# A rational activation in a fused attention and expert kernel: the absolute value moves behind a product, and unit 4 converts two weight chunks

## Chip, cores and metric

The kernel runs on one core of a Trainium2 chip. The metric is the device time of one execution in microseconds (us), as the median of several runs. Half a per cent of it is 3.1 us.

## What is computed

Causal attention over 4 batches, 12 heads, 448 positions and 64 dimensions gives x, of 1792 tokens and 768 features. On it follows a feed-forward layer with 2048 hidden features and a rational activation:

```python
h = x @ w_in
h2 = h * h
h3 = h2 * h
P = a[0] + a[1] * h + a[2] * h2 + a[3] * h3
Q = 1.0 + np.abs(b[0]) * np.abs(h) + np.abs(b[1]) * h2
g = P / (Q + 1e-06)
return (g @ w_out).astype(np.float32)
```

The weights and a, b come as 64-bit floats, and the kernel itself turns the weights into 32-bit ones. Each matrix product is made of three passes over high and low halves of the operands (fp32r): high by high, high by low, low by high.

## The kernel before

**Stages.** The first 140 us or so are attention, worked in 24 pairs of heads from an order written out by hand (ORDER, FIRST). A second written order (TAIL) leads over into the expert layer, whose first two units it contains. From unit 2 on a loop (line 674) does the rest.

**Units.** The tokens are four chunks of 512, 512, 384 and 384 columns. A unit t is one token chunk with one block f of 128 hidden features; there are 64, in the order of w_units (line 94): chunk 0 with blocks 0 to 7 (units 0 to 7), chunk 1 with all 16 (units 8 to 23), chunk 0 with blocks 8 to 15 (units 24 to 31), then chunks 2 and 3.

- p1(t) (line 198): 18 matmuls into a PSUM tile h, two buffers deep.
- act_a(t) (line 436): ScalarE reads h three times: u = |h| (L441), w = |b1 h| (L442) and p, a linear function of h (L443).
- dve_a, dve_a3 (lines 446, 453): VectorE makes w = (w + |b0|) * u (L448), and p = p * h (L451), p = (p + ..) * h (L456); L456 is the last reader of h.
- act_b (line 460): the reciprocal on ScalarE as Ln (L463) and Exp (L466), into u.
- dve_b, dve_b3 (lines 468, 477): one Newton step and the product with p (L470, L473, L479).
- g_hi, g_lo (lines 483, 488): ScalarE casts the high half gh (L485), VectorE subtracts for the low half gl (L492).
- p2(t) (line 497): 24 matmuls (18 for the shorter chunks) into psO and psM. At the last unit of a token chunk the passes are sorted so that the results come out one after another, and gl is wanted early.

In TensorE's queue p1(t+1) stands ahead of p2(t-1) in turn t of the loop.

**Weights.** Each 64-bit block of 128 rows is a chunk of the conversion; there are 32, listed in items (line 111). conv_step makes a chunk in four steps: 1 on GpSimd (L135, into a buffer u, three deep), 2 on VectorE (L145), 4 on ScalarE (L143), 3 on VectorE (L151). A chunk's raw block has three buffers, and its load is asked for when the chunk three before it is done (conv_load after conv_store, line 717). Ten chunks are converted in the attention stage; from unit 2 on there is one per unit (line 673), so chunk m is converted in unit m - 8.

Before use a 32-bit block is split: w_hi casts on ScalarE (L179), w_lo subtracts (L187) on GpSimd for w_out blocks (n == 1) and on VectorE for w_in blocks. The w_in block of unit t + 3 is split at the end of turn t. The w_out block of unit t is split in turn t, and there are two places for it:

```python
                late = (w_units[t][1], 1) in [items[m] for m in now]
                if not late and t < NU - 2:
                    split_w(t, 1)
```

stands behind dve_a3 and ahead of act_b; a late one stands at line 714, behind the conversion's step 3 and dve_b3, ahead of split_w(t + 3, 0) and so ahead of g_hi(t) and g_lo(t), which the next turn issues. By items, chunks 13, 14, 15 are the w_out blocks 5, 6, 7, and chunks 29, 30, 31 are the w_out blocks 13, 14, 15: units 5, 6, 7 and 21, 22, 23 take the late place.

SP issues all DMAs in program order: the store of a converted chunk waits for its L151, the store of split halves (L190) for L187, loads of later weights (L166, L170) stand behind them.

Of the kernel before, what the change touches and what calls it, by code (L numbers as in the profile page):

```python
# [11 lines left out]
AF = mybir.ActivationFunctionType  # L12
ALU = mybir.AluOpType
# [27 lines left out]
def kernel(  # L41
# [11 lines left out]
    nc = tc.nc  # L53
# [29 lines left out]
    bb = const.tile([P, 2], F32, name="bb")  # L83
# [72 lines left out]
    def conv_store(m):  # L156
        nc.sync.dma_start(out=w32[items[m]], in_=c_32[m])
        stored.add(items[m])
# [37 lines left out]
    h_t = {}  # L196
# [41 lines left out]
    def half(j):  # L238
        return slice(j * D, (j + 1) * D)
# [176 lines left out]
    def parse(order):  # L416
        plan = []
        for w in order.split():
            name, _, lag = w.partition("@")
            name, *arg = name.split(".")  # L420
            plan.append((tasks[name], [int(x) for x in arg], int(lag) if lag else None))
        return plan
# [7 lines left out]
    NU = len(w_units)  # L430
    tmp, g_t, acc, osb, part = {}, {}, {}, {}, {}

    def n_of(t):
        return chunks[w_units[t][0]][1]

    def act_a(t):
        h, n = h_t[t], n_of(t)
        u = tp.tile([P, 512], F32, tag="u", name="u")[:, :n]
        w = tp.tile([P, 512], F32, tag="w", name="w")[:, :n]
        pp = tp.tile([P, 512], F32, tag="p", name="p")[:, :n]  # L440
        nc.scalar.activation(out=u, in_=h, func=AF.Abs)  # L441
        nc.scalar.activation(out=w, in_=h, func=AF.Abs, scale=bb[:, 1:2])  # L442
        nc.scalar.activation(out=pp, in_=h, func=AF.Identity, scale=na[:, 3:4], bias=na[:, 2:3])  # L443
        tmp[t] = (u, w, pp)

    def dve_a(t):
        u, w, pp = tmp[t]
        nc.vector.scalar_tensor_tensor(  # L448
            out=w, in0=w, scalar=bb[:, 0:1], in1=u, op0=ALU.add, op1=ALU.mult
        )  # L450
        nc.vector.tensor_tensor(out=pp, in0=pp, in1=h_t[t], op=ALU.mult)  # L451

# [7 lines left out]
    def act_b(t):  # L460
        u, w, pp = tmp[t]
        r = u
        nc.scalar.activation(  # L463
            out=r, in_=w, func=AF.Ln, scale=2.0 ** -LSH, bias=lnb[:, 0:1]
        )
        nc.scalar.activation(out=r, in_=r, func=AF.Exp, scale=-1.0, bias=lnb[:, 1:2])  # L466
# [10 lines left out]
    def dve_b3(t):  # L477
        w, pp = tmp[t][1:]
        nc.vector.scalar_tensor_tensor(  # L479
            out=pp, in0=w, scalar=2.0, in1=pp, op0=ALU.subtract, op1=ALU.mult  # L480
        )
# [94 lines left out]
    def coeffs():  # L576
        nc.sync.dma_start(out=ab[:, 0:4], in_=moe_a.partition_broadcast(P))
        nc.sync.dma_start(out=ab[:, 4:6], in_=moe_b.partition_broadcast(P))

    def coeffs_done():  # L580
        nc.vector.tensor_scalar_mul(na, ab[:, 0:4], -1.0)
        nc.scalar.activation(out=bb, in_=ab[:, 4:6], func=AF.Abs)
# [9 lines left out]
    with tc.manual_schedule():  # L592
        nc.scalar.preload_act_table_set("natural_log_exp_and_others")
        nc.vector.memset(lnb[:, 0:1], QC * 2.0 ** -LSH)
        nc.vector.memset(lnb[:, 1:2], -LSH * LN2)
        make_identity(nc, ident)


        es_l, es_r = ExitStack(), ExitStack()
        pool = tc.tile_pool  # L600
        ep = es_l.enter_context(pool(name="ep", bufs=1))
        at = es_l.enter_context(pool(name="at", bufs=1))
        sm = es_l.enter_context(pool(name="sm", bufs=4))
        lv = es_l.enter_context(pool(name="lv", bufs=2))
        ps_t = es_l.enter_context(pool(name="ps_t", bufs=1, space=PSUM))
        ld = es_r.enter_context(pool(name="ld", bufs=2, side="right"))
        qk = es_r.enter_context(pool(name="qk", bufs=2, side="right"))
        ps_s = es_r.enter_context(pool(name="ps_s", bufs=1, space=PSUM, side="right"))
        mask = qk.tile([P, S], F32, tag="mask", bufs=1, name="mask")
        nc.gpsimd.memset(mask, 0.0)  # L610
        for x in range(2):
            m = mask[half(x), S - QB:]
            nc.gpsimd.affine_select(
                out=m, in_=m, compare_op=ALU.is_ge, fill=-1e9 / SCALE, base=0, pattern=[[-1, QB]], channel_multiplier=1,
            )
        for x in ("x3", "d"):
            ps_s.tile([P, 512], F32, tag=x, name="psS")

        V = [lv.tile([P, 2, 4, D], F32, tag=f"v{x}", bufs=1, name=f"vraw{x}") for x in range(3)]
        E = [  # L620
            [ep.tile([P, min((w + P - 1) // P * P, S)], F32, tag=f"e{x}{i}", name=f"e{x}{i}") for i, w in enumerate(b_w)]
            for x in range(2)
        ]

        warm = E[1][6][:, :P]
        idle = ps_s.tile([P, 512], F32, tag="d", name="psI")[:, :P]
        for x in range(2):
            SUM[x] = sm.tile([P, NE, 2], F32, tag=f"sum{x}", bufs=1, name="sums")
            nc.gpsimd.memset(SUM[x][:, :, 1:], 1e-9)
        for x in range(3):  # L630
            nc.gpsimd.memset(V[x][:QB, :, 3], 0.0)
        for x in range(2):
            for e, w in zip(E[x], b_w):
                if w < e.shape[1]:
                    nc.gpsimd.memset(e[:, w:], 0.0)

        nc.vector.memset(warm, 0.0)

        def keep_warm(n):
            for _ in range(n):  # L640
                nc.tensor.matmul(idle, warm, warm, start=True, stop=True, skip_group_check=True)

        keep_warm(8)

        def attend(p, part):
            for fn, arg, lag in part:
                if 0 <= p - lag < NP:
                    fn(p - lag, *arg)

        for fn, arg, p in parse(HEAD):  # L650
            fn(*arg) if p is None else fn(p, *arg)
        for p in range(NHEAD, NP):
            if p == 2:
                coeffs()
            if p == 6:
                coeffs_done()
            if p in (1, 2, 3):
                conv_load((1, 2, 3).index(p))
            attend(p, (first, second)[p] if p in (0, 1) else plan)
            if 0 <= p - NP + 4 < NL:  # L660
                conv_store(p - NP + 4)
            if p == NP - 2:
                split_w(0, 0)
            if p == NP - 2:
                load_w(0, 1)
            if p == NP - 1:
                load_w(3, 0)
                load_w(1, 1)

        for fn, arg, lag in parse(TAIL):  # L670
            fn(*arg) if lag is None else fn(NP - lag, *arg)
        todo = list(range(NC, len(items)))
        step = {t: [todo.pop(0) for _ in range(1) if todo] for t in range(2, NU)}
        for t in range(2, NU + 1):
            now = step.get(t, [])
            if t < NU - 2:
                p1(t + 1)
            g_hi(t - 1)
            g_lo(t - 1)
            if t < NU:  # L680
                dve_a(t)
                dve_a3(t)
                for m in now[:1]:
                    conv_step(m, 2)
# [3 lines that stand above are left out]
                if t + 4 < NU and splits(t + 4, 0):  # L688
                    load_w(t + 4, 0)
                if t + 3 < NU and not splits(t + 3, 0):  # L690
                    load_w(t + 3, 0)
                act_b(t)
                for m in now:
                    conv_step(m, 4)
            if t == NU - 3:
                p1(NU - 1)
            ahead = 1 < t < NU and w_units[t - 1][0] != w_units[t][0]
            if ahead:
                dve_b(t)
                dve_b3(t)  # L700
            p2(t - 1)
            if t + 1 < NU:
                act_a(t + 1)
            if NU - 2 <= t < NU:
                split_w(t, 1)
            if t < NU:
                if not ahead:
                    dve_b(t)
                for m in now[:1]:
                    conv_step(m, 3)  # L710
                if not ahead:
                    dve_b3(t)
            if t < NU and late:
                split_w(t, 1)
            if t + 3 < NU:
                split_w(t + 3, 0)
            for m in now:
                conv_store(m)
                conv_load(m + NR)
            load_w(t + 2, 1)  # L720
            for m in step.get(t + 1, []):
                conv_step(m, 1)
# [32 lines left out]
```

## Time and profile before

| | us |
|---|---|
| median of 3 runs | 629.04 |
| lowest and highest | 626.59, 629.29 |
| the profiled execution | 627.17 |
| its span, first to last instruction | 625.4 |

| engine | busy share of the span |
|---|---|
| TensorE, matmuls | 98% |
| VectorE | 83% |
| ScalarE | 69% |
| GpSimd | 29% |

In the rows below PE is TensorE's matmuls, DVE VectorE, ACT ScalarE, POOL GpSimd. L448 is line 448 of the kernel. Busy shares are averages over stages: attention up to some 140 us, the units with conversion up to some 360 us, and the rest. "out<-in" gives the tiles by their names in the program; psH is h of p1, psO and psM the two parts of p2's output, whl a split weight. [...]

### The profile page before, as it was taken

Reading aid. Unit: us, or ns where it says so; the run is one execution under the profiler, and the core shown is the slowest. Engines: PE = TensorE matmul, PEld = TensorE weight load, DVE = VectorE, ACT = ScalarE, POOL = GpSimd, SP = SyncE. Lnnn points to the kernel's source line nnn. Section 1 sums busy time; section 2 is a strip of 40 time slices with the busy share of each in tenths; the row PEclk is TensorE's granted clock in tenths of the full one; section 3 lists DMA queues with packets and bytes.
Section 4 is the critical chain, followed back from the end, with each engine's and each line's share of the span. In section 5 each row is a group of like instructions: output and inputs, shape, how many; then the busy total and the mean of one; then the engine's idle time right before and its main releaser. Section 6 shows DMA issues by size and latency. Waiting matters only on the chain.

```text
span 625.4 us, 13037 instructions
## 1 busy us (share of the span) xinstructions
PE 612.3 (98%) x4728; PEld 515.8 (82%) x4728; DVE 516.1 (83%) x1039; ACT 429.7 (69%) x940; POOL 184.3 (29%) x251
## 2 busy tenths in 40 slices
PE   7999999999999989999999999999999999999997
PEld 5666677767888768888888788899999999999996
DVE  4799999995999999999998888678766566876664
ACT  5999999996776666668776575555654555755453
POOL 3688888885643231213442300000000000000000
PEclk9899999999999989999999999999999999999999
DMA  8898888895565789888975699547477767567763
GB/s 167 227 210 189 219 205 207 220 249 170 203 252 202 273 298 323 291 303 301 324 265 214 259 373 339 211 153 288 138 249 255 271 207 255 193 201 253 253 202 126
DMA packets 108897, 149.10 MB, mean 238 GB/s; under 512 B 70945, under 2 KB 83361, under 8 KB 108833
## 3 DMA queue, kind: packets, MB, share of 16 engines
q1 hardware_dynamic: 108832, 148.27, 73.2%
q8 instruction: 37, 0.61, 0.4%
q14 instruction: 28, 0.22, 0.1%
HBM read 111.28 MB, written 36.96 MB: 237 GB/s over the span
## 4 chain that ended last, share of the span: by engine, by line
PE 76%; DVE 11%; ACT 7%; issue 4%; POOL 1%; DMA 1%; ACTq 0%; DVEq 0%; POOLq 0%
PE psH L204 29%; PE psO L528 20%; PE psM L524 11%; PE psS L288 6%; PE psD L366 5%; PE psC L342 3%; ACT e L309 3%; DVE whl L187 2%; ACT whl L179 2%; PE psA L256 2%; DVE u L145 2%; DVE gl L492 1%; DVE w L448 1%; DVE u L151 1%; DVE p L473 1%
## 5 line engine op out<-in xcount | busy, mean ns | idle before, releaser
L204 PE MATMUL psH<-xh,whl 128*128 128x512 f32 (+1 forms) x768 | 176.1, 364 | 0.5 <-DVE p L456 0.4
L528 PE MATMUL psO<-whl,gh 128*128 128x512 f32 x448 | 160.5, 394 | 1.6 <-ACT gh L485 1.5
L204 PEld LDWEIGHTS psH<-xh,whl 128*128 128x128 f32 x768 | 136.0, 188 | 16.6 <-DVE p L456 1.0
L524 PE MATMUL psM<-whl,gh 128*128 128x256 f32 x448 | 126.5, 283 | 0.0
L463 ACT ACTIVATE u<-w,lnb 128x512 f32<-128x512 f32 (+1 forms) x64 | 42.9, 671 | 105.1 <-DVE w L448 105.1
L528 PEld LDWEIGHTS psO<-whl,gh 128*128 128x128 f32 x448 | 84.5, 189 | 20.3 <-ACT gh L485 2.6
L204 PE MATMUL psH<-xl,whl 128*128 128x512 f32 (+1 forms) x384 | 87.5, 362 | 0.0
L323 POOL TENSOR_SCALAR e<-e,r 128x192 f32<-128x192 f32 (+6 forms) x168 | 77.2, 483 | 32.5 <-DVE r L319 15.4
L524 PEld LDWEIGHTS psM<-whl,gh 128*128 128x128 f32 x448 | 85.0, 190 | 1.4
L528 PE MATMUL psO<-whl,gl 128*128 128x512 f32 x224 | 81.7, 393 | 2.3 <-DVE gl L492 2.3
L309 ACT ACTIVATE e<-psS,nm 128x448 f32<-128x448 f32 (+6 forms) x168 | 77.4, 485 | 4.5 <-DVE nm L299 3.8
L204 PEld LDWEIGHTS psH<-xl,whl 128*128 128x128 f32 x384 | 70.1, 188 | 7.6
L187 DVE TENSOR_TENSOR whl<-w,whl 128x768 fp32r<-128x768 f32 x41 | 47.1, 1149 | 30.8 <-ACT whl L179 30.8
L492 DVE TENSOR_TENSOR gl<-p,gh 128x384 fp32r<-128x384 f32 (+1 forms) x62 | 41.6, 671 | 35.0 <-ACT gh L485 35.0
L441 ACT ACTIVATE u<-psH 128x512 f32<-128x512 f32 (+1 forms) x64 | 34.5, 539 | 48.8 <-PE psH L204 48.7
L299 DVE CUSTOM_DVE_ANT_0 psS<-psS,mask 128x64 f32<-128x64 f32 (+6 forms) x168 | 65.2, 453 | 2.8 <-PE psS L288 2.8
L524 PE MATMUL psM<-whl,gl 128*128 128x256 f32 x224 | 63.4, 283 | 0.0
L135 POOL TENSOR_SCALAR u<-raw 128x768 f32<-128x768 f32 x32 | 48.3, 1510 | 43.5 <-DMA raw<-in_moe_w_in_dram 16.4
L470 DVE SCALAR_TENSOR_TENSOR w<-w,u 128x512 f32<-128x512 f32 (+1 forms) x64 | 46.4, 724 | 11.3 <-ACT u L466 11.3
L448 DVE SCALAR_TENSOR_TENSOR w<-w,bb,u 128x512 f32<-128x512 f32 (+1 forms) x64 | 46.4, 725 | 6.7 <-ACT w L442 6.7
L528 PEld LDWEIGHTS psO<-whl,gl 128*128 128x128 f32 x224 | 42.3, 189 | 11.7 <-DVE gl L492 2.9
L288 PE MATMUL psS<-qkt 64*64 64x192 f32 (+6 forms) x672 | 48.7, 395 | 1.9 <-ACT e L309 1.6
(64 smaller groups left out, 992.9 us busy)
## 6 DMA issues: line engine op xcount, KB each, us to landing
whl<-whl SPq DMA_DIRECT2D x88, 768.0 KB, 4.3
w<-w SPq DMA_DIRECT2D x52, 384.0 KB, 5.4
raw<-in_moe_w_in_dram SPq DMA_DIRECT2D x16, 768.0 KB, 5.7
raw<-in_moe_w_out_dram SPq DMA_DIRECT2D x16, 768.0 KB, 4.9
w<-u SPq DMA_DIRECT2D x29, 384.0 KB, 3.4
qraw<-in_q_dram SPq DMA_DIRECT2D x48, 112.0 KB, 3.8
kraw<-in_k_dram SPq DMA_DIRECT2D x48, 112.0 KB, 3.8
out_dram<-osb SPq DMA_DIRECT2D x13, 384.0 KB, 2.9
```

Source lines behind the costliest of these rows:

```text
L135: nc.gpsimd.tensor_scalar(out=u.bitcast(F32), in0=y, scalar1=0.0, scalar2=1.0, op0=ALU.mult, op1=ALU.mult)
L187: eng.tensor_tensor(out=w[:, 1], in0=src, in1=w[:, 0].bitcast(F32), op=ALU.subtract)
L204: nc.tensor.matmul(ps, w[:, c * P:(c + 1) * P], x[c][:, lo:lo + n_tok], start=(c == 0 and n == 0), stop=(c == KD - 1 and n == 2),)
L288: nc.tensor.matmul(pss[p, b][half((1 + b + j) % 2)], QK[p][half(j), 0, b * QB:(b + 1) * QB], QK[p][half(j), 1, :b_w[b]], start=True, stop= ...
L299: nc.vector.tensor_tensor_reduce(out=s, in0=s, in1=mask[:, S - w:], scale=-SCALE, scalar=3e38, op0=ALU.add, op1=ALU.min, accum_out=nmx[p][ ...
L309: nc.scalar.activation(out=E[p % 2][i][:, :w], in_=pss[p, i], func=AF.Exp, bias=nmx[p][:, i:i + 1], scale=-1.0, accum_out=SUM[p % 2][:, i, ...
L323: nc.gpsimd.tensor_scalar(out=e, in0=e, scalar1=REC[p][:, i:i + 1], scalar2=0.0, op0=ALU.mult, op1=ALU.add)
L448: nc.vector.scalar_tensor_tensor(out=w, in0=w, scalar=bb[:, 0:1], in1=u, op0=ALU.add, op1=ALU.mult)
L470: nc.vector.scalar_tensor_tensor(out=w, in0=w, scalar=QC, in1=r, op0=ALU.add, op1=ALU.mult)
L492: eng.tensor_tensor(out=gl, in0=pp, in1=gh.bitcast(F32), op=ALU.subtract)
L524: nc.tensor.matmul(acc["m", k], g, w[:, 512:], start=first and (k % 2 == 0 or nk < 4), stop=last, skip_group_check=True)
L528: nc.tensor.matmul(acc[k], g, w[:, :512], start=first, stop=last)
```

## The change

act_a no longer makes u = |h|. L448 multiplies (w + |b0|) by h itself, read from PSUM, and ScalarE takes the absolute value of that product, in place, ahead of the logarithm: (|b1 h| + |b0|) |h| is the absolute value of (|b1 h| + |b0|) h. Unit 4 gets two chunks to convert, so that every chunk from 13 on is converted one unit earlier, and the last in unit 22 where it was 23. The second chunk's steps on VectorE (2 and 3) stand behind dve_b3 of unit 4; its step 1 on GpSimd follows the first one's at the end of unit 3, and its step 4 on ScalarE the first one's.

```diff
@@ act_a
-        nc.scalar.activation(out=u, in_=h, func=AF.Abs)
         nc.scalar.activation(out=w, in_=h, func=AF.Abs, scale=bb[:, 1:2])
@@ dve_a
-            out=w, in0=w, scalar=bb[:, 0:1], in1=u, op0=ALU.add, op1=ALU.mult
+            out=w, in0=w, scalar=bb[:, 0:1], in1=h_t[t], op0=ALU.add, op1=ALU.mult
@@ act_b
         r = u
+        nc.scalar.activation(out=w, in_=w, func=AF.Abs)
@@ the loop over units
-        step = {t: [todo.pop(0) for _ in range(1) if todo] for t in range(2, NU)}
+        step = {t: [todo.pop(0) for _ in range(1 + (t == 4)) if todo] for t in range(2, NU)}
...
                 if not ahead:
                     dve_b3(t)
+                for m in now[1:]:
+                    for n in (2, 3):
+                        conv_step(m, n)
             if t < NU and late:
                 split_w(t, 1)
```

## Rows read from the trace of the kernel before

**Rows 1.** Chain of waits: start us, us, engine, tile and line; psH blocks.
```profile
245.40 4.09 PE psH L204 x18
...
328.00 4.11 PE psH L204 x18
...
362.12 4.09 PE psH L204 x18
```
**Rows 2.** TensorE's timeline, 197 to 230 us: start, duration, instruction [idle before, releaser].
```profile
197.28 1.53 PE L204 MATMUL psH<-xh,whl 128*128 128x512 f32 x6
...
201.38 0.39 PE L528 MATMUL psO<-whl,gh 128*128 128x512 f32 x1
...
210.83 0.50 PE L528 MATMUL psO<-whl,gh 128*128 128x512 f32 x1 [0.74 <-ACT gh L485]
...
215.63 1.66 PE L204 MATMUL psH<-xh,whl 128*128 128x512 f32 x6 [0.36 <-DVE p L456]
...
223.55 0.50 PE L528 MATMUL psO<-whl,gl 128*128 128x512 f32 x1 [1.47 <-DVE gl L492]
...
224.73 0.63 PE L528 MATMUL psO<-whl,gl 128*128 128x512 f32 x1
...
228.69 1.55 PE L204 MATMUL psH<-xh,whl 128*128 128x512 f32 x6
```
**Rows 3.** Windows: busy PE, PEld, DVE, ACT, POOL; granted clock, DMA share, GB/s.
```profile
225.00:250.00 25.00, 25.00 (x120) 21.20 (x120) 24.59 (x35) 18.01 (x29) 3.91 (x3) 0.94 0.89 310
```
**Rows 4.** VectorE's timeline, units 5 to 10.
```profile
193.53 0.74 DVE L448 SCALAR_TENSOR_TENSOR w<-w,bb,u 128x512 f32<-128x512 f32 x1
...
200.30 2.03 DVE L187 TENSOR_TENSOR whl<-w,whl 128x768 fp32r<-128x768 f32 x1 [1.04 <-ACT whl L179]
...
203.54 0.74 DVE L448 SCALAR_TENSOR_TENSOR w<-w,bb,u 128x512 f32<-128x512 f32 x1
...
223.42 1.36 DVE L448 SCALAR_TENSOR_TENSOR w<-w,bb,u 128x512 f32<-128x512 f32 x1
...
233.33 0.74 DVE L448 SCALAR_TENSOR_TENSOR w<-w,bb,u 128x512 f32<-128x512 f32 x1
...
241.15 0.74 DVE L448 SCALAR_TENSOR_TENSOR w<-w,bb,u 128x512 f32<-128x512 f32 x1
...
243.18 0.95 DVE L145 SCALAR_TENSOR_TENSOR u<-raw,u 128x768 uint32<-128x768 uint32 x1
244.05 0.69 DVE L470 SCALAR_TENSOR_TENSOR w<-w,u 128x512 f32<-128x512 f32 x1
```
**Rows 5.** ScalarE's timeline: gh of units 5 and 9, Exp of unit 10.
```profile
200.17 0.61 ACT L485 CAST gh<-p 128x512 fp32r<-128x512 f32 x1
...
239.78 0.62 ACT L485 CAST gh<-p 128x512 fp32r<-128x512 f32 x1 [0.89 <-DVE p L479]
...
242.74 0.72 ACT L466 ACTIVATE u<-u,lnb 128x512 f32<-128x512 f32 x1
```
**Rows 6.** GpSimd's timeline: the late subtraction of unit 5.
```profile
199.67 1.85 POOL L187 TENSOR_TENSOR whl<-u,whl 128x768 fp32r<-128x768 f32 x1 [10.60 <-issue]
```
**Rows 7.** Views of lines 448 and 456: ns min/median/max, first and last start, forms.
```profile
L448 DVE SCALAR_TENSOR_TENSOR w<-w,bb,u x64: 609/674/1881, 147.9 to 613.1; 128x512 f32<-128x512 f32 x32, 128x384 f32<-128x384 f32 x32
...
L456 DVE SCALAR_TENSOR_TENSOR p<-p,na,psH x64: 614/674/751, 150.6 to 614.3; 128x512 f32<-128x512 f32 x32, 128x384 f32<-128x384 f32 x32
```
**Rows 8.** Groups by line and form: xcount, busy us, mean ns, idle before.
```profile
L485 ACT CAST gh<-p 128x512 fp32r<-128x512 f32 x32 | 20.0, 625 | 13.0 <-DVE p L479 12.9
...
L441 ACT ACTIVATE u<-psH 128x512 f32<-128x512 f32 x32 | 18.8, 589 | 12.4 <-PE psH L204 12.4
...
L593 ACT ACT_TABLE_LOAD x1 | 1.3, 1283 | 0.7 <-PEq L737 0.7
```
**Rows 9.** Timelines of ScalarE and TensorE in the last unit: gh and its use.
```profile
616.93 0.52 ACT L485 CAST gh<-p 128x384 fp32r<-128x384 f32 x1 [1.81 <-DVE p L479]
...
618.27 0.39 PE L528 MATMUL psO<-whl,gh 128*128 128x512 f32 x1
```

## Prediction

> **What bounds the kernel now.** I read first the chain of waits, then TensorE's timeline and the windows, then the timelines of the engines that feed it. TensorE is busy nearly everywhere after the attention stage, so a microsecond counts only where TensorE itself is late. Its own pitch in the expert stage comes from the chain of waits: blocks of 18 psH matmuls start at 245.40 and 328.00, ten units apart, so 8.26 us per unit of 512 tokens [rows 1]. Against that pitch there are two places where it loses time.
>
> The first is units 5 to 7. The psH block that starts at 197.28 is followed three units later by the one at 228.69 [rows 2]: 31.41 us where 3 x 8.26 = 24.78 were needed, a loss of **6.63 us**. The reader should see in the same rows what TensorE waited for: 0.74 us for gh (ScalarE), 0.36 for psH to be freed (VectorE p), 1.47 for gl (VectorE), and then a stretch in which one psO matmul takes 0.63 instead of 0.39 us. [...]
>
> The second is the end of chunk 1: from 328.00 to 362.12 is 34.12 us for four units, which need 33.04 [rows 1], a loss of **1.08 us**.
>
> Behind both is one pattern. In VectorE's timeline L448 opens a unit: 193.53, 203.54, ... 223.42 (units 5, 6, 8), so 9.96 us per unit on the mean of three, against 233.33 to 241.15 = 7.82 in unit 9 [rows 4]. In unit 5 VectorE stood idle 1.04 us for ScalarE's high half of a weight (L179), and then its own L187 took 2.03 us. ScalarE issued gh, for which TensorE waited, only after that, at 200.17 [rows 5]. GpSimd's L187 ran from 199.67 to 201.52 [rows 6], and VectorE's L187, begun at 200.30, ended 0.8 us after it: VectorE waited until GpSimd was through. Operations with an operand in PSUM aren't held so: the longest of 64 L456 took 0.75 us, the longest L448, which has both operands in SBUF, 1.88 [rows 7]. All this is the "late" branch: the chunk converted in unit t is the very w_out block that unit t splits, so its split stands at the unit's end, ahead of gh and gl. It holds in units 5, 6, 7 and, by the same order of chunks, in 21, 22, 23, where the second loss lies.
>
> **The change, part by part.**
>
> *One chunk more in unit 4.* From then on each chunk is converted one unit earlier, so "late" is false in units 5 to 7 and 21 to 23, and the w_out split goes behind L456 of its unit. The loss of 6.63 and that of 1.08 are what can be had: 7.71 us. ScalarE then makes gh directly behind one cast, and GpSimd's subtraction falls beside L448, L451 and L456.
>
> What it costs: unit 4 gets two more VectorE instructions (shift-or, 0.87 from start to start: 243.18 to 244.05 [rows 4]), 1.74 us, one more ScalarE scaling of the chunk and one more GpSimd pass. VectorE's unit 5 then starts at 193.53 + 1.74 = 195.27. From L448 to the start of gh a unit without the late branch takes 239.78 - 233.33 = 6.45 us [rows 4, 5]; with the cast's 0.62 and 0.1 for the longer round trip below, gh of unit 5 is ready at 195.27 + 7.2 = 202.4. TensorE wants it at 201.38 [rows 2]. So a **stall of 1.0 us** stays, once: the following VectorE units take some 7.9 us against TensorE's 8.26, and catch up. Bounds: 0, if the first units gain a microsecond because L448 no longer waits for GpSimd (the 1.36 us of the L448 at 223.42 is such a wait [rows 4]); 2.0, if the second GpSimd pass in unit 4 and the early subtraction each hold VectorE 0.5 us.
>
> Queues that the moved work passes: GpSimd does the extra pass ahead of unit 4's weight subtraction, and it needs the u buffer of a chunk whose last reader is VectorE's L187 at the end of unit 3. That subtraction may so be a microsecond late; it is wanted in TensorE's second pass only, and its gh slack hides it. On SP, the store of the second chunk waits for its L151, and the next raw load and the loads of unit 5 stand behind it, some 2 us; those weights are used two and more units later (over 16 us), so I take 0. Every raw load is asked for one unit earlier, the first of them with one unit (8 us) of lead where there were two. Lost cover would hold GpSimd, not TensorE.
>
> *The absolute value behind the product.* ScalarE does as many operations as before, but one of them now stands between VectorE's L448 and the logarithm. Its price isn't in the trace: the nearest rows are the absolute value from PSUM, 0.59 us, and the cast from SBUF to SBUF, 0.625 [rows 8]; I take 0.62, the row whose operands both lie in SBUF, as they will. Today Exp ends at 242.74 + 0.72 = 243.46 and VectorE comes to L470 at 244.05 [rows 4, 5]: 0.59 us of slack, so VectorE waits about 0.1 us more per converting unit. Its period goes from 7.82 to some 7.9, still under 8.26: nothing on the path. In units without conversion VectorE is idle for microseconds each unit.
>
> *L448 reads h from PSUM.* L456 is the same operation with that operand: the shortest of each, for 384 columns, took 614 and 609 ns [rows 7], so +5 ns; 0 on the path. h's buffer is freed by L456 as before. [...]
>
> *The last unit* has two round trips in a row. gh starts at 616.93 and TensorE wants it at 618.27 [rows 9]; less its 0.52 that is 0.8 us of slack, which two Abs (some 0.5 each for 384 columns) less the earlier start of the first (0.4) use up nearly. Cost 0, bound 0.3.
>
> **Sum.** 6.63 - 1.0 + 1.08 = 6.7 us less. The profiled execution took 627.17 us with a span of 625.4, so 620.5 for its like; it lies 1.87 us under the median of 629.04. I give the median: 629.04 - 6.7 = **622.3 us**.
>
> **Rivals.**
>
> *A, the lock moves along.* GpSimd's early subtraction meets VectorE's SBUF operations in units 5 to 7 all the same, about 1.1 us each (the 2.03 of that L187, less 0.95 for the instruction of the same size at 243.18 [rows 4]), of which 0.36 is caught up, and the stretch at the lower clock (about 1.5 us of the 6.63: five pairs of matmuls at 0.65 in place of 0.35) comes back. Then 1.0 + 3 x 0.74 + 1.5 = 4.7 us are lost in place of 1.0, the gain is 3.0, and the time 626.0. For it: VectorE has little idle time in these units. Against it: L448, L451, L456 stand next to each other and the subtraction starts with them.
>
> *B, ScalarE's queue in unit 4 takes the place.* The second scaling waits for GpSimd's second pass, and that for a raw block loaded one unit before and for a u buffer. Behind it on ScalarE stand act_a of unit 5, the cast for unit 7 and gh of unit 4, and TensorE waits for gh. Each microsecond by which the second scaling comes late beyond gh's slack is a microsecond off the gain; 4 to 7 us late would leave 626 to 629. For it: nothing else in the loop is held by two units' buffers at once. Against it: a raw block asked for one unit ahead has 8 us, and nothing in rows 2 waits for a load.
>
> *C, slower: the round trip becomes the bound.* Place: L470 waiting for Exp in units 2 to 22. It decides when Abs costs more than 0.59 + 0.44 = 1.03 us, for then VectorE's period passes 8.26. Each 0.1 us above costs 21 x 0.1 = 2.1 us, so that an Abs of 1.5 us would turn the gain into a loss of 3. With a table load of 1.28 us ahead of each Abs [rows 8] it would cost 0.62 + 1.28 - 1.03 = 0.87 a unit, 18.3 us, less the 6.7 gained: 640.6. Against it: Abs runs today between Ln and Exp with one table load in the whole kernel.
>
> *D, the change does not remove the late branch.* It compares the unit's own w_out block with the chunks of that unit; after the shift no unit after 4 converts its own block. I see no room.
>
> **How the numbers follow.** My case 0.72 (619 to 624), A 0.13, B 0.10, C 0.05. The lower end is the lowest run, 626.59, less 7.7; the upper takes in A: **619.0 to 626.5**. Half a per cent (3.1 us) is about what a measurement of this kernel can tell from no change. Faster by more: my case and half of A, 0.79; within: the other half and most of B, 0.15; slower: 0.06.
>
> **What would show it.** Right: L448 to L448 of 8.0 or so in units 5 to 7 and about 10 in unit 4; no idle VectorE before L187 at their ends; one TensorE stall near 201, under 2 us; psH starts 8.26 apart from there to chunk 2; a granted clock of 1.00 in 225 to 250; in ScalarE's chain Abs, Ln, Exp with Abs near 0.62 us and VectorE's wait before L470 up by some 0.1 us. Wrong: TensorE stalls in units 6 to 8, L470 waiting over 0.5 us in converting units, or a table load more.

## The result, and the profile after

The median went from 628.21 us (four runs, 626.59 to 629.29) to **620.55 us** (four runs, 618.99 to 622.75): 7.66 us less, a ratio of 0.988 with a 95% interval of 0.984 to 0.992. The forecast was 622.3 in a range of 619.0 to 626.5, so the time lies 1.75 us below the forecast; 0.83 of that is the kernel before, whose median was 629.04 when the forecast was made from it. The profiled execution took 620.98 us.

Line numbers moved a little: the product, L448 of before, is L447, L456 is L455, and the new absolute value is L462. First the head of the page, the span and the busy time of each engine:

```profile
span 619.2 us, 12979 instructions
...
PE 608.9 (98%) x4728; PEld 514.5 (83%) x4728; DVE 501.9 (81%) x1039; ACT 439.7 (71%) x940; POOL 171.9 (28%) x251
```

TensorE is still the engine that bounds the kernel. Its timeline from the psH block of unit 7 to that of unit 10 answers to [rows 2] (start, duration, instruction, idle time before it and what ended that); the last line is from the last unit and is read further down:

```profile
198.00 1.53 PE L204 MATMUL psH<-xh,whl 128*128 128x512 f32 x6
...
202.73 0.50 PE L528 MATMUL psO<-whl,gh 128*128 128x512 f32 x1 [0.48 <-ACT gh L485]
...
207.00 1.53 PE L204 MATMUL psH<-xh,whl 128*128 128x512 f32 x6
...
215.26 1.53 PE L204 MATMUL psH<-xh,whl 128*128 128x512 f32 x6
...
223.52 1.53 PE L204 MATMUL psH<-xh,whl 128*128 128x512 f32 x6
...
612.00 0.39 PE L528 MATMUL psO<-whl,gh 128*128 128x512 f32 x1
```

From 198.00 to 223.52 three units take 25.52 us where 24.78 are needed: a loss of 0.74 in place of 6.63, and the wait for gh at 202.73 is the only one between 185 and 235 us. The windows show the clock that goes with it (columns as in [rows 3]):

```profile
200.00:225.00 25.00, 24.52 (x125) 20.67 (x125) 24.86 (x34) 19.09 (x29) 7.37 (x6) 1.00 0.96 343
225.00:250.00 25.00, 25.00 (x128) 21.11 (x127) 24.45 (x34) 18.48 (x28) 3.77 (x4) 1.00 0.82 289
```

The granted clock is 1.00 in 225 to 250 where it was 0.94 [rows 3]; in 225 to 228 it is 1.00 where the trace of before shows 0.50, with matmuls of psO that take 0.63 us in place of 0.39. TensorE is busy all the 25 us in both. At the end of chunk 1, in the chain of waits:

```profile
331.29 4.09 PE psH L204 x18
...
364.33 4.09 PE psH L204 x18
```

Four units take 33.04 us, just what they need; before it was 34.12 [rows 1]. VectorE's timeline shows why TensorE no longer waits:

```profile
148.83 0.75 DVE L447 SCALAR_TENSOR_TENSOR w<-w,bb,psH 128x512 f32<-128x512 f32 x1 [4.41 <-ACT p L442]
...
185.47 0.73 DVE L447 SCALAR_TENSOR_TENSOR w<-w,bb,psH 128x512 f32<-128x512 f32 x1
...
195.67 0.74 DVE L447 SCALAR_TENSOR_TENSOR w<-w,bb,psH 128x512 f32<-128x512 f32 x1
...
197.71 1.58 DVE L145 SCALAR_TENSOR_TENSOR u<-raw,u 128x768 uint32<-128x768 uint32 x1
...
201.95 0.94 DVE L187 TENSOR_TENSOR whl<-w,whl 128x768 fp32r<-128x768 f32 x1
...
203.42 0.74 DVE L447 SCALAR_TENSOR_TENSOR w<-w,bb,psH 128x512 f32<-128x512 f32 x1
...
211.16 0.73 DVE L447 SCALAR_TENSOR_TENSOR w<-w,bb,psH 128x512 f32<-128x512 f32 x1
...
219.53 0.73 DVE L447 SCALAR_TENSOR_TENSOR w<-w,bb,psH 128x512 f32<-128x512 f32 x1
```

Unit 4 takes 10.20 us (185.47 to 195.67), units 5, 6 and 7 take 7.75, 7.74 and 8.37, where they took about 9.96 [rows 4]. The L187 at the end of unit 5 runs 0.94 us with no idle time ahead of it, where it had 1.04 idle and 2.03 busy. GpSimd's subtraction now stands early in the unit:

```profile
195.24 2.24 POOL L187 TENSOR_TENSOR whl<-u,whl 128x768 fp32r<-128x768 f32 x1 [5.57 <-ACT whl L179]
197.59 0.89 POOL L135 TENSOR_SCALAR u<-raw 128x768 f32<-128x768 f32 x1
```

It runs beside L447 (195.67, not held, 0.74 us) and lasts to 197.48; the conversion pass L135 behind it meets VectorE's L145 (197.71, 1.58 us in place of 0.95). Last, the ScalarE chain with the new step, and the last unit:

```profile
196.44 0.63 ACT L462 ACTIVATE w<-w 128x512 f32<-128x512 f32 x1 [1.29 <-DVE w L447]
197.11 0.72 ACT L463 ACTIVATE u<-w,lnb 128x512 f32<-128x512 f32 x1
197.87 0.73 ACT L466 ACTIVATE u<-u,lnb 128x512 f32<-128x512 f32 x1
...
202.06 0.62 ACT L485 CAST gh<-p 128x512 fp32r<-128x512 f32 x1 [0.69 <-DVE p L479]
...
611.26 0.51 ACT L485 CAST gh<-p 128x384 fp32r<-128x384 f32 x1 [1.80 <-DVE p L479]
```

Exp ends at 198.60, and VectorE's L470 begins at 199.21, behind L145. In the last unit gh is ready at 611.26 + 0.51 = 611.77, and TensorE takes it at 612.00 (above): 0.23 us of slack where [rows 9] had 0.82, and no stall.

For comparing profiles one needs a measure without the attention stage, whose end varies: the first psH block started between 141.69 and 149.07 us in the profiles of this study, of whatever kernel. From that start to the end of the span, "the expert stage" below, the kernel before takes 625.4 - 142.31 = 483.1 us and the changed one 619.2 - 143.01 = 476.2, **6.9 us** less; the forecast was 6.7. The distance between psH blocks is sharper still.

### The profile page after: what moved, and what is told of

It reads as the page before. It is cut to its first block, busy times and chain, and to the rows that moved or that the text cites. A ratio compares the mean times of both kernels' runs of the same rounds, so it can differ in the third digit from the quotient of the medians.

```text
span 619.2 us, 12979 instructions
## 1 busy us (share of the span) xinstructions
PE 608.9 (98%) x4728; PEld 514.5 (83%) x4728; DVE 501.9 (81%) x1039; ACT 439.7 (71%) x940; POOL 171.9 (28%) x251
## 4 chain that ended last, share of the span: by engine, by line
PE 84%; DVE 5%; issue 3%; POOL 3%; DMA 2%; ACT 2%; SPq 0%; POOLq 0%; DVEq 0%; ACTq 0%
PE psH L204 32%; PE psO L528 23%; PE psM L524 12%; PE psS L288 6%; PE psD L366 5%; PE psC L342 4%; PE psA L256 2%; POOL e L323 1%; POOL whl L187 1%; DVE u L145 1%; DMA w<-w 1%; DMA vraw<-in_v_dram 1%; PE psI L641 1%; DVE at L354 1%; ACT e L309 1%
## 5 line engine op out<-in xcount | busy, mean ns | idle before, releaser
L462 ACT ACTIVATE w<-w 128x512 f32<-128x512 f32 (+1 forms) x64 | 37.1, 580 | 82.9 <-DVE w L447 82.9
L441 ACT ACTIVATE w<-psH,bb 128x512 f32<-128x512 f32 (+1 forms) x64 | 40.3, 630 | 45.3 <-PE psH L204 45.3
L470 DVE SCALAR_TENSOR_TENSOR w<-w,u 128x512 f32<-128x512 f32 (+1 forms) x64 | 41.8, 653 | 37.0 <-ACT u L466 37.0
L492 DVE TENSOR_TENSOR gl<-p,gh 128x384 fp32r<-128x384 f32 (+1 forms) x62 | 38.2, 617 | 25.9 <-ACT gh L485 25.9
L187 DVE TENSOR_TENSOR whl<-w,whl 128x768 fp32r<-128x768 f32 x42 | 41.5, 988 | 18.4 <-ACT whl L179 17.8
L135 POOL TENSOR_SCALAR u<-raw 128x768 f32<-128x768 f32 x32 | 38.7, 1210 | 53.8 <-DMA raw<-in_moe_w_out_dram 29.4
L485 ACT CAST gh<-p 128x512 fp32r<-128x512 f32 (+1 forms) x64 | 36.4, 568 | 18.0 <-DVE p L479 17.9
```

Source lines behind the costliest of these rows:

```text
L135: nc.gpsimd.tensor_scalar(out=u.bitcast(F32), in0=y, scalar1=0.0, scalar2=1.0, op0=ALU.mult, op1=ALU.mult)
L187: eng.tensor_tensor(out=w[:, 1], in0=src, in1=w[:, 0].bitcast(F32), op=ALU.subtract)
L470: nc.vector.scalar_tensor_tensor(out=w, in0=w, scalar=QC, in1=r, op0=ALU.add, op1=ALU.mult)
L492: eng.tensor_tensor(out=gl, in0=pp, in1=gh.bitcast(F32), op=ALU.subtract)
```

## The experiments

Ratios are to the kernel before, run on the same chip. None of the kernels leaves out or alters what is computed; e3, e6 and e9 take one absolute value more than they need, and e8 one that nothing reads. Where an edit adds a line, the lines behind it count one higher than in the changed kernel (the product is L448 in e3, e8 and e9, L470 is L471 in e6).

**e1, the extra chunk alone.** The product stays as it was, so this is the kernel before with

```diff
-        step = {t: [todo.pop(0) for _ in range(1) if todo] for t in range(2, NU)}
+        step = {t: [todo.pop(0) for _ in range(1 + (t == 4)) if todo] for t in range(2, NU)}
...
+                for m in now[1:]:
+                    for n in (2, 3):
+                        conv_step(m, n)
```

> The change's second part alone: unit 4 converts two chunks, the absolute value stays where it was (u = |h| on ScalarE, VectorE multiplies by u). Theory 1 (the place of the w_out split makes the gain): the time is within 1.5 us of the changed kernel, 620.5 to 622; TensorE loses 0.7 to 2.5 us over units 5 to 7 (197.28 to 228.69 of the kernel before became 31.41 us; expected 25.5 to 27.3) and nothing in units 21 to 23. Theory 2 (the early split helps only because L447 now has an operand in PSUM and GpSimd's subtraction runs beside it): VectorE's first operation of units 5 to 7 is held by GpSimd for about 1 us each, the stalls stay, and the time is 624 to 626.

Measured: 623.4 us, ratio 0.994 [0.992, 0.996], between the expectations. TensorE's blocks from 191.23 to 228.16 take 36.93 us for four units of 8.26, a loss of 3.89 in one place; the expert stage is 3.8 us shorter than before. The place is the psH block of unit 7, in TensorE's timeline:

```profile
201.68 2.77 PE L204 MATMUL psH<-xh,whl 128*128 128x512 f32 x6 [1.82 <-DVE p L456]
```

It comes 2.19 us late, of which 1.82 are spent waiting for L456 to free psH. The other 1.70 us are lost behind it: its first six matmuls take 2.77 us in place of 1.53, and the window 200 to 225 has a granted clock of 0.93. L456 was late since L448 ahead of it was held in unit 5, as VectorE's timeline shows:

```profile
197.89 2.35 DVE L448 SCALAR_TENSOR_TENSOR w<-w,bb,u 128x512 f32<-128x512 f32 x1
...
206.62 0.75 DVE L448 SCALAR_TENSOR_TENSOR w<-w,bb,u 128x512 f32<-128x512 f32 x1
```

GpSimd's timeline gives the reason:

```profile
197.46 2.24 POOL L187 TENSOR_TENSOR whl<-u,whl 128x768 fp32r<-128x768 f32 x1 [5.56 <-ACT whl L179]
...
206.70 2.38 POOL L187 TENSOR_TENSOR whl<-u,whl 128x768 fp32r<-128x768 f32 x1 [5.61 <-DVE gl L492]
```

In unit 5 GpSimd was first by 0.43 us, and L448 lasted until GpSimd had finished. In unit 6 VectorE was first by 0.08, and its L448 took the usual 0.75. In these two units it was decided by who came first.

**e2, the absolute value and the PSUM operand alone** (the changed kernel with both parts of the diff above taken back).

```diff
-        step = {t: [todo.pop(0) for _ in range(1 + (t == 4)) if todo] for t in range(2, NU)}
+        step = {t: [todo.pop(0) for _ in range(1) if todo] for t in range(2, NU)}
...
-                for m in now[1:]:
-                    for n in (2, 3):
-                        conv_step(m, n)
```

> The change's first part alone: h read from PSUM by VectorE, absolute value behind the product, one chunk per unit as before. Theory 1: the late splits of units 5 to 7 and 21 to 23 stay, the loss of TensorE over units 5 to 7 is 5 to 6.6 us, and the time is within 1.5 us of the kernel before, 626.5 to 629.5. Theory 2: freeing VectorE's first operation from GpSimd is worth 0.7 us or more in each of units 2 to 8; the loss falls to 3 us or less and the time to 624 to 625.5. If the longer round trip costs (rival C of the prediction), it is slower than before by 1 us or more.

Measured: 626.16 us, ratio 0.998 [0.996, 1.000]. The blocks at 198.05, 206.31, 215.93 and 227.47 leave a loss of 4.64 in place of 6.63; 0.50 follows in the next unit, and 0.68 at the end of chunk 1. VectorE's timeline keeps the late pattern, without the hold of the product that [rows 4] has at 223.42:

```profile
220.56 2.01 DVE L187 TENSOR_TENSOR whl<-w,whl 128x768 fp32r<-128x768 f32 x1 [1.03 <-ACT whl L179]
223.76 0.73 DVE L447 SCALAR_TENSOR_TENSOR w<-w,bb,psH 128x512 f32<-128x512 f32 x1
```

So this part helps by itself a little: 2.2 us of the expert stage in the profiled executions, while the medians differ by 1.2 us and their interval ends at 1.000. The parts alone give 3.8 + 2.2 = 6.0, together 6.9.

**e4, the place of the split alone.** The changed kernel, but the split of w_out is put back to the end of units 5 to 7 and 21 to 23, though its chunk is there early:

```diff
-                late = (w_units[t][1], 1) in [items[m] for m in now]
+                late = t in (5, 6, 7, 21, 22, 23)
```

> The changed kernel with the w_out split of units 5, 6, 7, 21, 22, 23 put back at its late place by hand, though the chunk is there a unit earlier. Theory 1 (the place): the loss comes back, 5.5 to 8 us over units 5 to 7 (unit 4 still has the second chunk) and about 1 us at the end of chunk 1, the clock falls to its lower level for some 3 us near 225, and the time is 626 to 629. Theory 3 (it is the earlier conversion itself, data that is there in time): VectorE has no wait for the chunk, the loss stays under 2 us and the time under 623.

Measured: 626.25 us, ratio 0.997 [0.995, 1.000]. TensorE's timeline:

```profile
208.57 1.66 PE L204 MATMUL psH<-xh,whl 128*128 128x512 f32 x6 [0.39 <-DVE p L455]
...
218.18 1.64 PE L204 MATMUL psH<-xh,whl 128*128 128x512 f32 x6 [0.36 <-DVE p L455]
```

From 199.09 to 230.90 three units take 31.81, a loss of 7.03: with the early chunk but the late place the stall is all there. The granted clock in the window is 0.93, where the kernel before had 0.94 and the changed kernel 1.00:

```profile
225.00:250.00 25.00, 24.25 (x116) 20.73 (x117) 24.11 (x34) 17.85 (x28) 4.87 (x5) 0.93 0.83 306
```

It is therefore the place in the unit, ahead of gh and gl, that costs the 6.6 us, not the conversion beside it. The loss at the end of chunk 1 did not come back, against the expectation: its four units take 33.04 us. In the kernel before, TensorE's timeline has one wait there, for gl of unit 23:

```profile
358.38 0.50 PE L528 MATMUL psO<-whl,gl 128*128 128x512 f32 x1 [0.80 <-DVE gl L492]
```

With the chunks one unit earlier, unit 23 converts nothing: in e4 VectorE does it in 8.20 us (349.42 to 357.62, L447 to L447) where the kernel before needs 9.31 (348.94 to 358.25), and this wait is gone though the split stands late. So the early place isn't what gains the 1.08 us; the earlier conversion does it together with the early place (e1: 33.04 us for the four units) or with the operand in PSUM (e4). By itself it was not run.

**e3, the product's operand back in SBUF.** The changed kernel, with |h| made again and read by the product:

```diff
+        nc.scalar.activation(out=u, in_=h, func=AF.Abs)
...
-            out=w, in0=w, scalar=bb[:, 0:1], in1=h_t[t], op0=ALU.add, op1=ALU.mult
+            out=w, in0=w, scalar=bb[:, 0:1], in1=u, op0=ALU.add, op1=ALU.mult
```

> The changed kernel, with u = |h| made on ScalarE as before and multiplied from SBUF, and the second absolute value kept, so that only the place of VectorE's second operand goes back (ScalarE does one operation more per unit, about 0.5 us of its idle time). If the PSUM operand matters by the lock between VectorE and GpSimd: the longest of VectorE's first operations is again over 1.2 us (0.75 in the changed kernel), the loss in units 5 to 7 is 1.2 to 3 us in place of 0.74, and the time is 0.5 to 2 us over the changed kernel's 620.55. If it does not matter: the loss stays under 1 us and the time within 0.5 us.

Measured: 633.24 us, ratio 1.009 [1.006, 1.012]: slower than the kernel before, and far outside what I had expected. VectorE and GpSimd in units 6 and 7:

```profile
207.27 2.34 DVE L448 SCALAR_TENSOR_TENSOR w<-w,bb,u 128x512 f32<-128x512 f32 x1
...
216.55 2.34 DVE L448 SCALAR_TENSOR_TENSOR w<-w,bb,u 128x512 f32<-128x512 f32 x1
```

```profile
207.10 1.96 POOL L187 TENSOR_TENSOR whl<-u,whl 128x768 fp32r<-128x768 f32 x1 [6.01 <-ACT whl L179]
...
216.38 1.96 POOL L187 TENSOR_TENSOR whl<-u,whl 128x768 fp32r<-128x768 f32 x1 [6.00 <-ACT whl L179]
```

GpSimd is first by 0.17 us in each of them, the product is held for 1.6 us each time, and TensorE's blocks stand 9.23 to 9.28 us apart (211.04, 220.32, 229.55, 238.80) in place of 8.26. Two causes were left, as e3 also gives ScalarE an operation more.

**e8, that operation alone.** The changed kernel with the first of e3's three edits: |h| is made, and the product reads PSUM.

```diff
+        nc.scalar.activation(out=u, in_=h, func=AF.Abs)
```

> The changed kernel with u = |h| made on ScalarE once more, and used by nobody (the logarithm writes over it): ScalarE has the same operations as in the run with the operand from SBUF, which took 633.24 us with TensorE's blocks 9.28 us apart in units 7 to 10 and 21 to 24; only L447's second operand is h in PSUM. Theory (VectorE's first operation, with both operands in SBUF, was held there by GpSimd's subtraction for 1.6 us a unit): no block pitch over 8.5 us after unit 6, L447 never over 0.8 us, time within 1.5 us of the changed kernel, 620 to 622.5. Rival (ScalarE's fourth operation is what makes 9.28): the pitch stays over 9 us in those units and the time is 630 or more.

Measured: 621.35 us, ratio 0.990 [0.987, 0.994], like the changed kernel itself, run once more as e5 (no edit, on another chip): 621.09 us, 0.991 [0.988, 0.993]. For e5 this stood on record:

> The changed kernel once more, as the measure for the two runs beside it: 619 to 623 us, TensorE's loss over units 5 to 7 0.5 to 1.0 us.

The view of e8's product line (shortest, median, longest in ns, first and last start):

```profile
L448 DVE SCALAR_TENSOR_TENSOR w<-w,bb,psH x64: 604/670/748, 155.4 to 614.2; 128x512 f32<-128x512 f32 x32, 128x384 f32<-128x384 f32 x32
```

Not one of 64 is held. Only the operand differs between e3 and e8, so e3's 12 us need it in SBUF; the extra operation on ScalarE costs nothing that the times show. The operand alone doesn't make 12 us: e1 has it in SBUF too and took 623.4 us. From unit 5 on, GpSimd's subtraction is ahead of the product in two units of e1 (5 and 20) and in eleven of e3 (5 to 7 and 16 to 23). Beyond e1, e3 has the absolute value behind the product; that this step shifts who comes first is likely, and was not tested by itself.

**e9, e3 with the split moved behind Exp,** where the product can't meet it:

```diff
-                if not late and t < NU - 2:
-                    split_w(t, 1)
...
+                if not late and t < NU - 2:
+                    split_w(t, 1)
```

> The run with the operand from SBUF (633.24 us), with the w_out split moved behind the exponential on ScalarE, so that GpSimd's subtraction can't start ahead of VectorE's first operation of the unit. Theory (which of the two engines starts first decides; in that run GpSimd was ahead by 0.17 us and VectorE waited out the whole subtraction, in the run with the two chunks alone VectorE was ahead by 0.08 us in units 6 and 7): the first operation is no longer held (none over 1.4 us after unit 4), the 9.28 us pitch is gone, and the time falls to 621 to 626, since the subtraction now meets VectorE's later operations. Rival (the subtraction costs VectorE its whole length wherever it stands, or the other operand is slow by itself): the pitch stays over 9 us, and the time over 630.

Measured: 636.82 us, ratio 1.013 [1.008, 1.018]: the time that the rival gave, and not the 621 to 626 of the theory. The product is free, but the hold has moved, as VectorE's and GpSimd's timelines show:

```profile
210.91 0.74 DVE L448 SCALAR_TENSOR_TENSOR w<-w,bb,u 128x512 f32<-128x512 f32 x1
...
215.40 2.33 DVE L151 SCALAR_TENSOR_TENSOR u<-raw,u 128x768 uint32<-128x768 uint32 x1 [0.19 <-ACT raw L143]
217.66 1.36 DVE L480 SCALAR_TENSOR_TENSOR p<-w,p 128x512 f32<-128x512 f32 x1
```

```profile
214.63 2.29 POOL L187 TENSOR_TENSOR whl<-u,whl 128x768 fp32r<-128x768 f32 x1 [5.66 <-DVE w L471]
```

In neither of the two places that were tried did GpSimd's subtraction leave free the VectorE operations beside it that read two operands from SBUF (2.34 us for the product in e3, 2.33 for L151 here); the products that read PSUM (the changed kernel, e8) took 0.75 us at the most.

**e6, how much room the round trip has left.** A second absolute value on w, in the chain:

```diff
         nc.scalar.activation(out=w, in_=w, func=AF.Abs)
+        nc.scalar.activation(out=w, in_=w, func=AF.Abs)
```

> The changed kernel with the absolute value behind the product taken twice, which adds one more step of about 0.66 us to the round trip from VectorE's product to the reciprocal, and nothing to VectorE's own work. Theory (the round trip has 0.5 us of slack in converting units, and VectorE's units may grow from 7.74 to 8.26 us before TensorE feels it): VectorE waits about 0.5 us more ahead of L470 in converting units, its units take 8.1 to 8.4 us, TensorE loses 0.5 to 2.5 us more than in the changed kernel and the time is 621 to 623. Rival C (the round trip is already the bound): every 0.66 us counts in 20 units, the time is over 627.

Measured: 624.01 us, ratio 0.995 [0.993, 0.997], 2.9 us above e5 on the same chip and somewhat more than expected. VectorE's timeline in unit 9, then TensorE's in unit 8 and in the last unit:

```profile
230.14 0.74 DVE L447 SCALAR_TENSOR_TENSOR w<-w,bb,psH 128x512 f32<-128x512 f32 x1
...
233.76 0.69 DVE L471 SCALAR_TENSOR_TENSOR w<-w,u 128x512 f32<-128x512 f32 x1 [0.63 <-ACT u L467]
...
238.60 0.73 DVE L447 SCALAR_TENSOR_TENSOR w<-w,bb,psH 128x512 f32<-128x512 f32 x1
```

```profile
229.14 0.50 PE L529 MATMUL psO<-whl,gh 128*128 128x512 f32 x1 [0.89 <-ACT gh L486]
...
614.89 0.50 PE L529 MATMUL psO<-whl,gh 128*128 128x512 f32 x1 [0.78 <-ACT gh L486]
```

In units 8 to 15 the whole second Abs becomes a wait, 0.63 us, and unit 9 takes 8.46 us (230.14 to 238.60), over TensorE's 8.26. The first Abs fitted the slack there; a second doesn't. But not every unit pays: units 16 to 21, where L145 runs beside GpSimd's L135 (in the changed kernel it takes 1.43 to 1.62 us there, 0.95 in units 9 to 14), have no wait ahead of L471 and take 7.85 to 7.87 us. TensorE waits for gh where the changed kernel doesn't in units 2, 8 and 9 (0.84, 0.89, 0.26 us) and in the last unit, where the changed kernel had 0.23 us of slack and this one waits 0.78.

**e7, a stall of VectorE in unit 2.** In the changed kernel L470 of unit 2 waits 2.09 us for Exp, which stands behind the split's cast on ScalarE. Here Exp goes first in that unit:

```diff
+                if t == 2:
+                    act_b(t)
                 if not late and t < NU - 2:
...
-                act_b(t)
+                if t != 2:
+                    act_b(t)
```

> The changed kernel with one thing moved: in unit 2 ScalarE does the absolute value, logarithm and exponential ahead of the cast of that unit's w_out block, which waits for its load. In the changed kernel VectorE stands idle 2.09 us there behind that cast. Theory (the stall that is left in unit 5 is VectorE's lateness, and it is summed up from unit 2): VectorE reaches unit 5 1 us or more earlier, TensorE's stall at unit 5 (0.48 us of waiting, 0.74 of loss) is gone, and the time is 0.7 us under the changed kernel's. Rival (the idle time hides other work: GpSimd's subtraction, which comes later by this, holds VectorE instead): the stall stays within 0.3 us of what it was, and so does the time.

Measured: 620.22 us, ratio 0.990 [0.987, 0.993], the lowest median of the study but within the interval of e5, which shared its chip. VectorE's timeline:

```profile
169.47 0.70 DVE L470 SCALAR_TENSOR_TENSOR w<-w,u 128x512 f32<-128x512 f32 x1
...
171.00 2.35 DVE L151 SCALAR_TENSOR_TENSOR u<-raw,u 128x768 uint32<-128x768 uint32 x1 [0.18 <-ACT raw L143]
```

The wait is gone, and 1.4 us of it comes back as a hold of L151 (0.94 us otherwise) by GpSimd's subtraction, which ran from 170.24 to 172.54. VectorE so reaches unit 5 only 0.3 us earlier, counted from the first psH block (194.04 - 141.69 = 52.35 us, against 195.67 - 143.01 = 52.66). The loss between TensorE's blocks went from 0.74 to 25.26 - 24.78 = 0.48, which is what the rival expected. That a quarter of a microsecond was won is likely from the blocks, and not shown by the times.

## Why the prediction was right, and which term was mis-sized

*The late branch goes.* Right, and in the amounts given: 6.63 - 0.74 + 1.08 = 6.97 us between the blocks, less 0.23 at the block after them, so 6.74 against the 6.7 of the sum. e4 confirms the cause by itself for units 5 to 7. For the 1.08 us at the end of chunk 1 the size was right and the cause was not: the prediction put it down to the late place too, and e4 has the late place without the loss. There it is the conversion that ends a unit earlier (e4 and e1, above).

*Unit 4 and the one stall.* Unit 4 grew from 193.53 - 185.06 (the L448 that opens it in the trace of before) = 8.47 to 10.20, by 1.73 us; forecast 1.74. gh of unit 5 was ready at 202.06 + 0.62 = 202.68; forecast 202.4, with an attention stage that ended 0.7 later. The stall was 0.48 us, or 0.74 by the blocks, where 1.0 stood in the sum: from L447 to the end of gh it took 7.0 us, not 7.2, and TensorE itself came later. Units 5 to 7 then took 7.75, 7.74 and 8.37 us, 7.95 on the mean, where the step said some 7.9.

*The round trip.* Right in price: by form, the new line and the table loads are

```profile
L462 ACT ACTIVATE w<-w 128x512 f32<-128x512 f32 x32 | 20.3, 634 | 36.9 <-DVE w L447 36.9
...
L593 ACT ACT_TABLE_LOAD x1 | 1.3, 1283 | 0.7 <-PEq L740 0.7
```

0.634 us for the 0.62 taken, and one table load as before, so rival C's dear case didn't arise. I had expected 0.1 us more of waiting at L470. In units 9 to 14 it starts 0.91 or 0.92 us after L145, where it was 0.87, so 0.05 us; in unit 5 GpSimd's L135 holds the L145 ahead of it for 0.63 us and so covers the trip. What lies beyond C's point was a miss of its own: its price was a lengthening of 0.1 us per 0.1 us over an Abs of 1.03, that is 21 x 0.24 = 5.0 us for two Abs of 1.27 together; e6 gave 2.9. The place holds, the number of units that pay is smaller, and the last unit, which C left out, pays as well; where the cost sets in one run can't tell.

*Rivals A and B.* B left no trace: no gh of unit 4 was waited for. A is the interesting one. Its mechanism, the hold that moves along with the subtraction, is what happened where the operand stayed in SBUF (a product of 2.35 us in e1, of 2.34 in e3), and e1's loss of 3.89 is near A's 4.7.

*The mis-sized term* is the step "L448 reads h from PSUM", which the sum had at "0 on the path". I priced the instruction, rightly: the view of its line reads

```profile
L447 DVE SCALAR_TENSOR_TENSOR w<-w,bb,psH x64: 606/671/748, 148.8 to 607.0; 128x512 f32<-128x512 f32 x32, 128x384 f32<-128x384 f32 x32
```

with 606 ns for the shortest where the SBUF form had 609 [rows 7]. But its worth lies in what did not hold it: the longest is 748 ns, where L448 reached 1881. [Rows 7] showed this, and the prediction used it only for the stall's lower bound and, without a price, in naming L448 against rival A. With the early chunk alone (e1) the loss is 3.89, with the operand in PSUM as well 0.74: **about 3.1 us of the 6.9 belong to a term that the sum held at nothing**, when it is added last; added first (e2) it brings 2.2. These are single profiles; the ratios, 0.994 for e1 against 0.988 and 0.991 for the changed kernel, put it at 2 to 3.5 us. The sum came out right since the 5.6 us that it gave to the early split already supposed that VectorE runs free, which the split alone doesn't give. Without the operand the forecast would have had to be rival A's.

The median's 7.66 us against the expert stage's 6.9 is within what the attention stage scatters.

## What to carry to other kernels

Beside GpSimd's subtraction the product with both operands in SBUF took up to 2.35 us (e1), and the one that reads h from PSUM 0.75 at the most, in 64 of the changed kernel. So where VectorE and GpSimd share a stage, try GpSimd's SBUF work beside VectorE operations that read an operand from PSUM, and price an operand's place by what can hold the instruction, not by its own duration. An operation queued at the end of a unit ahead of what TensorE consumes next can cost more than it lasts, as here (in e4 7.03 us over units 5 to 7 for three subtractions of some 2 us, and nothing at the end of chunk 1); preparing its input one unit earlier lets it move, and one longer unit pays for all later ones. For effects under a per cent read the distances between TensorE's blocks rather than the times.

## What was unexpected of the hardware

In these traces it was decided by who began first, down to leads of less than 0.1 us. In the kernel before, e1, e3 and e9, GpSimd's subtraction began ahead of a product with both operands in SBUF 21 times, by 0.04 to 1.35 us, and each of these products ended 0.54 or 0.55 us after the subtraction: a 0.74 us product took 2.34 us when GpSimd was 0.17 us ahead (e3), and 1.05 when it was 1.33 ahead (unit 0 of the kernel before). With VectorE ahead by 0.05 to 0.15 us (17 times) the product took 0.73 to 0.75, and GpSimd's operation 2.32 to 2.40 in place of 1.85. The product with one operand in PSUM went free in the changed kernel: 748 ns at the most, of 64, also with GpSimd's subtraction 0.43 us ahead (unit 5).

In unit 0 the product, which now reads PSUM, started at 148.83, after an idle time of 4.41 us that ended with ScalarE's L442, which makes p from the same h. The idle time itself is not new: units 0 and 1 had 4.21 and 2.50 us before, ended by w, which the product needs; now they have 4.41 and 2.68. New is that the product starts with the end of p, 0.7 us after w is made (L441, 147.44 + 0.69). The two runs that differ in the operand alone agree: in e3 the wait ends with w, in e8 with p. Whether the program asks for that order or the chip does, no run shows; it would count in a fuller stage.
